# Attention and two MLP stages on one core: split fp32r products for batches 0 and 1 and for ten slots of block 0

## The chip, the cores and the metric

The kernel runs on one core of a Trainium2 chip. The metric is device time in microseconds (us), from launch to end; the median of three runs of the kernel before is 1787.25 us (1786.49 to 1788.84). The core's engines are named as in the profile: PE is TensorE's matrix multiply and PEld its weight load, DVE is VectorE, ACT is ScalarE, POOL is GpSimd, SP is the engine that issues most DMAs.

## What is computed

Three stages follow one another: attention over pooled keys and values (8 batches, 8 heads, 576 rows, head size 64; pooling by 8 leaves 72 keys), a first MLP with a cosine gate, and a second MLP with a SiLU gate.

```python
k_p = k.reshape(B, H, Sp, 8, D).mean(axis=3)
v_p = v.reshape(B, H, Sp, 8, D).mean(axis=3)
scores = q @ k_p.T / sqrt(D)                     # softmax over 72 keys
x = softmax(scores) @ v_p                        # to 4608 tokens x 512
h = x @ w_in;  x = (h * cos(h)) @ w_out          # 512 -> 2048 -> 512
g = x @ w_gate                                   # 512 -> 1536
out = (silu(g) * (x @ w_val)) @ w_out2           # 1536 -> 512
```

All inputs are float32 or float64 on the host and the output is float32. The MLP weights arrive as 64-bit words and are put together into float32 on the chip.

## The kernel before

**Two kinds of product.** A product in plain float32 is one matmul instruction, which the trace lists as two records. A split product writes each operand as a high part in fp32r (a rounded float32) and a low part, the remainder, and adds three matmuls: high by high, high by low, low by high. The high part is an ACT copy (`nc.scalar.copy`) and the low part a DVE subtraction.

**Blocks and slots.** The 4608 tokens are nine blocks of 512. Block n of the first MLP has 16 slots f, one for each 128 of the 2048 hidden rows. In a slot `pe_h` makes h with 12 split matmuls from `xhl` (the split input) and `wa` (split w_in), `turns` and `cosine` make g = h cos(h) in a tile `w` on ACT and DVE, `parts` splits g into `gh` and `gl` one slot later, and `pe_y` of two slots before adds g times w_out into four PSUM banks `acc`. A slot's h needs one of two PSUM banks, which the last DVE step of `cosine` (L573) two slots earlier frees. In block 0 the constant `Y32 = NF1 = 16` sends all slots down the plain path of `pe_y` (L599): four float32 matmuls from `w` and the float32 weights `wo_raw`, with no `parts`. From block 1 on `pe_y` has 12 split matmuls (L606 to L608), and `wo_high` (L553) and L586 make the split weights.

**Attention.** `do_s` makes scores, `do_pt` transposes the probabilities of a tile of 128 rows into `pth` (high), `ptl` (low) and `ptx` (the last 8 keys), `prep_v` makes the values' parts `vmh`, `vml`, `vl1`, `vl2`, and `do_av` multiplies them and ACT writes the result into `ring`. Batches below `ACTB = 2` take a plain float32 path: `do_av` has two float32 matmuls, `do_pt` no subtraction, `prep_v` no low parts. Later batches have five fp32r matmuls. Batch 0 is worked off ahead of the first slot (av of rows 0 to 511) and beside slots 0 and 1 (the last 64 rows); `x_split` makes `xhl` from `ring` as soon as it is there. Batch 1's attention runs beside slots 1 to 15, batch 2's beside block 1. Scores, transposes and av share the two PSUM banks tagged `att`.

**Weights and raw inputs.** `conv` turns the 64-bit words of w_in (tiles `st_i`, 16 of them) and w_out (`st_o`, 16) into float32: per tile one ACT scale (L477) and three DVE steps (L482, L487, L494), and for w_in a split (L1010 on ACT, L994 on DVE). It is called by `fill` all through the preamble and block 0. `load_kv1` loads batch 1's raw keys and values into tiles that belong to later weights: keys in `wa30` to `wa32`, values in `wa20` to `wa22`. DVE sums them (`pool_sum`, L213 and L215). SP issues all these loads in one order, and a load that waits for its tile holds up those behind it. Raw inputs of batch 2 and later are summed by POOL.

**Order.** The program is written slot by slot; a scheduler then sets each engine's order, except where `keep_in_program_order` pins an instruction (`x_split` of block 0, some transposes). Each engine works through its list strictly in that order.

Of the kernel before, what the change touches and what calls it, by code (L numbers as in the profile page):

```python
# [8 lines left out]
F32 = mybir.dt.float32  # L9
F32R = mybir.dt.float32r  # L10
# [15 lines left out]
def fused_kernel(  # L26
# [18 lines left out]
    nc = tc.nc  # L45
    B, H, S, D = q.shape
# [18 lines left out]
    PTW = 320  # L65
    LEAD = 4
    ACTB = 2
    Y32 = NF1

    const = ctx.enter_context(tc.tile_pool(name="const", bufs=1))  # L70
    chain = ctx.enter_context(tc.tile_pool(name="chain", bufs=2))
    dram = ctx.enter_context(tc.tile_pool(name="dram", bufs=1, space=bass.MemoryType.DRAM))
    psum = ctx.enter_context(tc.tile_pool(name="psum", bufs=1, space=bass.MemoryType.PSUM))
    wts = ctx.enter_context(tc.tile_pool(name="wts", bufs=1, reuse_waits="tile"))
    p1w = tc.alloc_tile_pool(name="p1w", bufs=2, side="right", reuse_waits="tile")
    p1a = tc.alloc_tile_pool(name="p1a", bufs=1, reuse_waits="tile")

    ident = const.tile([P, P], F32, name="ident")
# [5 lines left out]
    mask = few[:, 0]  # L84
# [20 lines left out]
    kT = p1a.tile([P, NP, 2 * SP], F32, name="kT")  # L105
    av_tiles = {}

    def av_tile(nm, b):

        kind = F32 if b < ACTB else F32R  # L110
        if (nm, kind) not in av_tiles:
            shape = {"v": [P, NP, P], "p": [P, NP, PTW], "x": [P, PTW]}["x" if nm == "ptx" else nm[0]]
            t = av_tiles[nm, kind] = p1a.tile(shape, kind, name=f"{nm}_{b}", tag=nm)
            if nm in ("vmh", "vml", "vl2"):
                nc.gpsimd.memset(t if kind is F32 else t.bitcast(F32), 0.0)
        return av_tiles[nm, kind]
# [50 lines left out]
    kraw1 = []  # L167
    vraw1 = []
# [19 lines left out]

    def load_kv1():

        for g in range(3):
            t = wts.tile([P, 2, TB], F32, name=f"k1_{g}", tag=f"wa3{g}")
            kraw1.append(t if g < 2 else t[: SL * NP])
            if g < 2:
                for x in range(2):
                    nc.sync.dma_start(t[x * SM : (x + 1) * SM], kview[1][g, x])
            else:
                for r in range(2):
                    nc.sync.dma_start(t[: SL * NP, r], kleft[1][r])
        for j in range(0, NP + 1, 2):  # L200
            t = wts.tile([P, 2, TB], F32, name=f"v1_{j}", tag=f"wa2{j // 2}")
            for r in range(2):
                rows = t[r * SM : (r + 1) * SM]
                if j < NP:
                    nc.sync.dma_start(rows, vview[1][r, :, j : j + 2])
                else:
                    nc.sync.dma_start(rows[:, 0], vleft[1])
            vraw1.append((j, t[:, : min(2, NP + 1 - j)]))

    def pool_sum(eng, dst, raw):  # L210
        h = POOL * D // 2
# [37 lines left out]
            nc.scalar.mul(to[:, :, SM:], ps[rows, 2 * P :].rearrange("d (s p) -> d p s", p=NP), -EXP_SCALE)  # L249

    def prep_v(b):
        vmh, vml, vl1, vl2 = (av_tile(nm, b) for nm in ("vmh", "vml", "vl1", "vl2"))
        vp = vps.pop(b)
        if b < ACTB:
            for r in range(2):
                rows, cols = slice(r * SM, (r + 1) * SM), slice(r * D, (r + 1) * D)
                nc.scalar.mul(vmh[rows, :, cols], vp[rows, :NP], 1.0 / POOL)
            nc.vector.tensor_mul(
                vl1[:SM].rearrange("q p (r d) -> q r p d", r=2),
                vp[:SM, NP : NP + 1].rearrange("q (a o) d -> q a o d", a=1).to_broadcast([SM, 2, NP, D]),  # L260
                mask[:SM].rearrange("q (p r o) -> q r p o", r=2, o=1).to_broadcast([SM, 2, NP, D]),
            )
            return
        for r in range(2):
            rows, cols = slice(r * SM, (r + 1) * SM), slice(r * D, (r + 1) * D)
            nc.scalar.mul(vmh[rows, :, cols], vp[rows, :NP], 1.0 / POOL)
            nc.vector.scalar_tensor_tensor(
                out=vml[rows, :, cols], in0=vp[rows, :NP], scalar=1.0 / POOL, in1=vmh[rows, :, cols],
                op0=ALU.mult, op1=ALU.subtract,
            )  # L270
        t = p1a.tile([P, H, SP], F32, name=f"vt_{b}", tag="e")[:, :, :D]
        nc.vector.tensor_mul(
            t, vp[:, NP : NP + 1].to_broadcast([P, H, D]), mask.rearrange("p (h o) -> p h o", o=1).to_broadcast([P, H, D])
        )
        t = t.rearrange("q (p r) d -> q r p d", r=2)
        h2 = vl1.rearrange("q p (r d) -> q r p d", r=2)
        l2 = vl2.rearrange("q p (r d) -> q r p d", r=2)
        for r in range(2):
            nc.scalar.copy(h2[:, r], t[:, r])
            nc.vector.tensor_sub(l2[:SM, r], t[:SM, r], h2[:SM, r])  # L280
# [49 lines left out]
    def do_norm(b, t, pm=None):  # L330
        n = TILES[t][1]
        e = es.pop((b, t))[:n]
        if b < ACTB:
            sm = sms.pop((b, t))[:n]
        else:
            sm = p1a.tile([P, H, 1], F32, name=f"sm_{b}_{t}", tag="sm", bufs=2)[:n]
            nc.vector.reduce_sum(sm[:, :, 0], e, axis=AX.X)
        nc.vector.tensor_scalar_add(sm, sm, 1e-9)
        nc.vector.reciprocal(sm, sm)
        if pm is None:  # L340
            pm = p1a.tile([P, H * SM + P], F32, name=f"pm_{b}_{t}", tag="pm")
        pms[b, t] = pm
        nc.vector.tensor_mul(
            pm[:n, : H * SM].rearrange("q (h s) -> q h s", h=H), e[:, :, :SM], sm.to_broadcast([n, H, SM])
        )

        for g in range(2):
            left = pm[:n, H * SM + g * SM : H * SM + (g + 1) * SM].rearrange("q (h s) -> q h s", h=H)
            if g == 0:
                nc.vector.tensor_mul(left, e[:, :, SM:], sm.to_broadcast([n, H, SL]))  # L350
            elif b >= ACTB:
                nc.vector.tensor_copy(pm[:n, H * SM + SM :], pm[:n, H * SM : H * SM + SM])

    def do_pt(b, t):
        pth, ptl, ptx = av_tile("pth", b), av_tile("ptl", b), av_tile("ptx", b)
        t0, n = TILES[t]
        o = t0 - GROUPS[GROUP[t]][0]
        pm = pms.pop((b, t))
        ps = psum.tile([P, NP, n], F32, name=f"pt_{b}_{t}", tag="att", bufs=2)
        for p in range(NP):  # L360
            pinned(nc.tensor.transpose(ps[:, p], pm[:n, p * P : (p + 1) * P], ident[:n, :n]), (b, t) == (0, 4))
        if b < ACTB:
            nc.scalar.copy(pth[:, :, o : o + n], ps)
            px = psum.tile([SM, n], F32, name=f"px_{b}_{t}", tag="att", bufs=2)
            nc.tensor.transpose(px, pm[:n, NP * P : NP * P + SM], ident[:n, :n])
            nc.scalar.copy(ptx[:SM, o : o + n], px)
            return
        nc.scalar.copy(pth[:, :, o : o + n], ps)
        nc.vector.tensor_sub(ptl[:, :, o : o + n], ps, pth[:, :, o : o + n])
        px = psum.tile([P, n], F32, name=f"px_{b}_{t}", tag="att", bufs=2)  # L370
        nc.tensor.transpose(px, pm[:n, NP * P :], ident[:n, :n])
        nc.scalar.copy(ptx[:, o : o + n], px)
        nc.vector.tensor_sub(ptx[SM:, o : o + n], px[SM:], ptx[SM:, o : o + n])

    def do_av(b, g, p):
        vmh, vml, vl1, vl2, pth, ptl, ptx = (
            av_tile(nm, b) for nm in ("vmh", "vml", "vl1", "vl2", "pth", "ptl", "ptx")
        )
        g0, n = (GROUPS if b else GROUPS0)[g]
        o = 256 if g == 2 else 0  # L380
        ps = psum.tile([P, n], F32, name=f"av_{b}_{g}_{p}", tag="att", bufs=2)
        terms = [
            (vmh, pth[:, p, o : o + n]),
            (vmh, ptl[:, p, o : o + n]),
            (vml, pth[:, p, o : o + n]),
            (vl1, ptx[:, o : o + n]),
            (vl2, ptx[:, o : o + n]),
        ]
        if b < ACTB:
            terms = [(vmh, pth[:, p, o : o + n])]  # L390
# [734 lines left out]
    for i, s in enumerate(slots):  # L1125
        n, f = s
# [157 lines left out]
```

## Time and profile before

| | us |
|---|---|
| median of three runs | 1787.25 |
| lowest, highest | 1786.49, 1788.84 |
| the profiled execution, its own time | 1786.07 |
| its span, first to last instruction | 1784.3 |
| PE busy | 1737.2 (97% of the span) |
| DVE busy | 1169.0 (66%) |
| ACT busy | 996.1 (56%) |
| POOL busy | 122.1 (7%) |

The profiled execution took 1.8 us more than its span. Busy times are instruction durations joined together; a PE matmul is shown from start to end, and the next one starts before it ends, so the distance between two starts tells more than a duration. PE idles for about 47 us of the span, nearly all of it in the first 130 us. The timelines list instructions of one engine with start, duration, line and tiles, and in brackets the idle time before one and what released it.

### The profile page before, as it was taken

To read this page: it belongs to the slowest core of one execution; us is meant where nothing else is said; L and a number is where in the kernel's file an instruction comes from. 1 tells how busy PE (TensorE), PEld (TensorE's weight loads), DVE (VectorE), ACT (ScalarE), POOL (GpSimd) and SP (SyncE) were. 2 spreads that over 40 slices of the span, in tenths; PEclk is the share of its full clock that TensorE was granted. 3 is DMA by queue.
4 is the path that set the end of the run, shared out by engine and by line. 5 is a ranking of instruction groups with operands and counts; after the bars stand their busy time and mean duration, and the time that the engine had idled before them with its cause. 6 is when DMAs were issued, how large, how long until landed. Compare 5 with 4: busy or idle time off the path is not lost.

```text
span 1784.3 us, 23241 instructions
## 1 busy us (share of the span) xinstructions
PE 1737.2 (97%) x8076; PEld 1444.5 (81%) x8076; DVE 1169.0 (66%) x2006; ACT 996.1 (56%) x1815; POOL 122.1 (7%) x217
## 2 busy tenths in 40 slices
PE   4979999999999999999999999999999999999998
PEld 3546588888888888888888778888888888999998
DVE  6695377867767677687675677853684377458346
ACT  5576477767667767677575565433443344344333
POOL 0131300403003011000000000000000000000000
PEclk9989999999999999999999999999999999999999
DMA  9553244646576455575775587675567657777772
GB/s 232 162 162 105 82 149 145 194 133 205 131 228 208 118 201 145 188 213 160 230 265 182 192 321 270 202 274 195 195 208 257 197 191 225 298 255 244 298 253 90
DMA packets 240244, 357.00 MB, mean 200 GB/s; under 512 B 141696, under 2 KB 147840, under 8 KB 240128
## 3 DMA queue, kind: packets, MB, share of 16 engines
q1 hardware_dynamic: 235440, 354.35, 61.5%
q10 hardware_dynamic: 4688, 1.18, 0.3%
q8 instruction: 64, 1.05, 0.2%
q14 instruction: 52, 0.43, 0.1%
HBM read 285.74 MB, written 69.73 MB: 199 GB/s over the span
## 4 chain that ended last, share of the span: by engine, by line
PE 89%; DMA 4%; DVE 4%; ACT 2%; issue 1%; POOL 0%; SPq 0%; ACTq 0%; DVEq 0%; POOLq 0%
PE X L791 14%; PE oX L921 8%; PE h L537 7%; PE h L538 7%; PE h L539 7%; PE acc L606 7%; PE Y L791 7%; PE acc L608 7%; PE acc L607 7%; PE oY L921 4%; PE av L393 3%; PE Z L791 3%; PE acc L599 2%; PE oZ L921 2%; PE s L308 2%; DMA w2r<-w_dram 1%
## 5 line engine op out<-in xcount | busy, mean ns | idle before, releaser
L791 PE MATMUL X<-t_P,wc 128*128 128x512 f32 (+1 forms) x1080 | 232.9, 368 | 2.3 <-ACT u L840 2.3
L537 PE MATMUL h<-xhl,wa 128*128 128x512 f32 x576 | 232.0, 403 | 1.3 <-DVE w L573 1.3
L539 PE MATMUL h<-xhl,wa 128*128 128x512 f32 x576 | 225.9, 392 | 0.0
L538 PE MATMUL h<-xhl,wa 128*128 128x512 f32 x576 | 225.9, 392 | 0.0
L791 PEld LDWEIGHTS X<-t_P,wc 128*128 128x128 f32 x1080 | 196.5, 188 | 29.1 <-ACT u L840 4.0
L606 PE MATMUL acc<-gh,wo_ring 128*128 128x512 f32 x448 | 179.3, 400 | 0.0
L607 PE MATMUL acc<-gl,wo_ring 128*128 128x512 f32 x448 | 174.8, 390 | 0.0
L608 PE MATMUL acc<-gh,wo_ring 128*128 128x512 f32 x448 | 174.8, 390 | 0.0
L547 ACT ACTIVATE w<-h,few 128x512 f32<-128x512 f32 x144 | 98.9, 687 | 121.3 <-PE h L539 121.0
L548 DVE SCALAR_TENSOR_TENSOR w<-w,h 128x512 f32<-128x512 f32 x144 | 98.2, 682 | 68.8 <-ACT w L547 68.5
L537 PEld LDWEIGHTS h<-xhl,wa 128*128 128x128 f32 x576 | 109.1, 189 | 27.8 <-issue 3.8
L573 DVE SCALAR_TENSOR_TENSOR w<-w,h 128x512 f32<-128x512 f32 x144 | 98.4, 683 | 49.9 <-ACT w L570 48.2
L538 PEld LDWEIGHTS h<-xhl,wa 128*128 128x128 f32 x576 | 108.9, 189 | 23.7 <-issue 2.4
L539 PEld LDWEIGHTS h<-xhl,wa 128*128 128x128 f32 x576 | 108.9, 189 | 23.0
L587 DVE TENSOR_TENSOR gl<-w,gh 128x512 fp32r<-128x512 f32 x128 | 90.9, 710 | 51.0 <-ACT gh L584 50.1
L584 ACT CAST gh<-w 128x512 fp32r<-128x512 f32 x128 | 78.9, 616 | 69.3 <-DVE w L573 47.3
L569 ACT ACTIVATE w<-w 128x512 f32<-128x512 f32 x144 | 91.1, 633 | 46.1 <-DVE w L548 45.1
L843 DVE TENSOR_TENSOR p<-p,X 128x512 f32<-128x512 f32 (+1 forms) x60 | 37.8, 632 | 116.8 <-PE X L791 108.6
L126 ACT CAST xhl<-pst 128x1024 fp32r<-128x1024 f32 (+1 forms) x70 | 67.7, 968 | 71.3 <-PE oX L921 26.1
L921 PE MATMUL oX<-xhl,wc 128*128 128x512 f32 (+1 forms) x480 | 102.7, 368 | 0.0
L608 PEld LDWEIGHTS acc<-gh,wo_ring 128*128 128x128 f32 x448 | 84.1, 188 | 18.6
L606 PEld LDWEIGHTS acc<-gh,wo_ring 128*128 128x128 f32 x448 | 84.2, 188 | 17.0 <-issue 0.8
(196 smaller groups left out, 3377.2 us busy)
## 6 DMA issues: line engine op xcount, KB each, us to landing
wc<-wc_dram SPq DMA_DIRECT2D x273, 512.0 KB
wo_ring<-wo_dram SPq DMA_DIRECT2D x112, 512.0 KB
wc_dram<-wc SPq DMA_DIRECT2D x42, 512.0 KB
wc_dram<-ow SPq DMA_DIRECT2D x42, 256.0 KB
y_dram<-yo SPq DMA_DIRECT2D x18, 512.0 KB
w_dram<-ce_w SPq DMA_DIRECT2D x36, 256.0 KB
st_i<-in_moe_w_in_dram SPq DMA_DIRECT2D x16, 512.0 KB
st_o<-in_moe_w_out_dram SPq DMA_DIRECT2D x16, 512.0 KB
```

Source lines behind the costliest of these rows:

```text
L537: nc.tensor.matmul(ps, whi, xhl[0][:, 0, c], start=c == 0, stop=False)
L538: nc.tensor.matmul(ps, whi, xhl[0][:, 1, c], start=False, stop=False)
L539: nc.tensor.matmul(ps, wlo, xhl[0][:, 0, c], start=False, stop=c == KC - 1)
L547: nc.scalar.activation(w, h, AF.Identity, bias=magic)
L548: nc.vector.scalar_tensor_tensor(out=w, in0=w, scalar=MAGIC, in1=h, op0=ALU.subtract, op1=ALU.subtract)
L569: nc.scalar.activation(w, w, AF.Sin, scale=PI)
L573: nc.vector.scalar_tensor_tensor(out=w, in0=w, scalar=1.0, in1=h, op0=ALU.subtract, op1=ALU.mult, reverse0=True)
L606: nc.tensor.matmul(acc[n][i], a[:, cols], xh, start=f == 0, stop=False)
L607: nc.tensor.matmul(acc[n][i], a[:, cols], xl, start=False, stop=False)
L608: nc.tensor.matmul(acc[n][i], b[:, cols], xh, start=False, stop=f == NF1 - 1)
L791: nc.tensor.matmul(ps[:, :hb], w, t[:, x, c, :hb], start=first and c == 0 and n == 0, stop=c == 1 and n == 2, skip_group_check=not first,)
L921: nc.tensor.matmul(banks[key][m][:, :hb], u, x[:, b, i, :hb], start=first_ and j == i == k == 0, stop=j == NJ - 1 and i == 1 and k == 2, s ...
```

## The change

`Y32` falls from 16 to 6: slots 6 to 15 of block 0 take the split path, with `wo_high`, `parts` and 12 matmuls each. The branches on `b < ACTB` go from `av_tile`, `prep_v`, `do_norm`, `do_pt` and `do_av`: batches 0 and 1 get the five-matmul av and all low parts. Their softmax keeps its own form. Batch 1's raw keys 0 and 1 move from `wa30` and `wa31` to the two `wo` buffers, and its values from `wa20` to `wa22` into the `gh` and `gl` buffers and `wa33`, one head pair a tile (ten loads of 128 KB in place of four of 256 and two of 128); the tiles `wo`, `gh` and `gl` are first written by `parts` of slot 6.

```diff
-    Y32 = NF1
+    Y32 = 6
@@ load_kv1
-        for g in range(3):
-            t = wts.tile([P, 2, TB], F32, name=f"k1_{g}", tag=f"wa3{g}")
...
+        for g in range(2):
+            t = p1w.tile([P, 2, TB], F32, name=f"k1_{g}", tag="wo", bufs=2)
...
+        t = wts.tile([P, 2, TB], F32, name="k1_2", tag="wa32")[: SL * NP]
...
-        for j in range(0, NP + 1, 2):
-            t = wts.tile([P, 2, TB], F32, name=f"v1_{j}", tag=f"wa2{j // 2}")
+        for j in range(NP + 1):
+            if j < NP:
+                t = chain.tile([P, 1, TB], F32, name=f"v1_{j}", tag="gh" if j < 2 else "gl", bufs=2)
             else:
+                t = wts.tile([P, 2, TB], F32, name=f"v1_{j}", tag="wa33")[:, :1]
@@ do_norm
-            elif b >= ACTB:
+            else:
                 nc.vector.tensor_copy(pm[:n, H * SM + SM :], pm[:n, H * SM : H * SM + SM])
@@ do_pt
-        if b < ACTB:
-            nc.scalar.copy(pth[:, :, o : o + n], ps)
-            px = psum.tile([SM, n], F32, name=f"px_{b}_{t}", tag="att", bufs=2)
-            nc.tensor.transpose(px, pm[:n, NP * P : NP * P + SM], ident[:n, :n])
-            nc.scalar.copy(ptx[:SM, o : o + n], px)
-            return
         nc.scalar.copy(pth[:, :, o : o + n], ps)
         nc.vector.tensor_sub(ptl[:, :, o : o + n], ps, pth[:, :, o : o + n])
@@ do_av
-        if b < ACTB:
-            terms = [(vmh, pth[:, p, o : o + n])]
-            terms += [(vl1[:SM], ptx[:SM, o : o + n])]
```

**PE, around the second product of slot 6.** Before, between batch 1's scores of tile 3 and h of slot 9:

```order
L308 MATMUL s_3_0_1062<-kT,qT_3_902 128x144 x2
L308 MATMUL s_3_1_1072<-kT,qT_3_902 128x144 x2
L599 MATMUL acc_0_696<-w_6_945,wo_449 128x512
L599 MATMUL acc_1_697<-w_6_945,wo_449 128x512
L599 MATMUL acc_2_698<-w_6_945,wo_449 128x512
L599 MATMUL acc_3_699<-w_6_945,wo_449 128x512
L293 MATMUL qp_4_1082<-ident,q_453 128x64 x4
```

After, from the same scores to the second of the four banks (the third and fourth follow in the same way; L586 to L588 are L606 to L608 of before):

```order
L297 MATMUL s_3_0_1172<-kT,qT_3_983 128x144 x2
L297 MATMUL s_3_1_1182<-kT,qT_3_983 128x144 x2
L586 MATMUL acc_0_766<-gh_6_1086,wo_6_1088 128x512
L587 MATMUL acc_0_766<-gl_6_1087,wo_6_1088 128x512
L588 MATMUL acc_0_766<-gh_6_1086,wo_6_1088 128x512
L586 MATMUL acc_1_767<-gh_6_1086,wo_6_1088 128x512
L587 MATMUL acc_1_767<-gl_6_1087,wo_6_1088 128x512
L588 MATMUL acc_1_767<-gh_6_1086,wo_6_1088 128x512
```

Four float32 matmuls from `w` and the raw weights became twelve fp32r matmuls from `gh`, `gl` and `wo`.

**DVE, in batch 0's attention ahead of the first slot.** Before, from the normalization of tile 1 (its probabilities lie in `vst`) to the score minima of tile 3:

```order
L343 TENSOR_TENSOR vst<-vst,sm_1_240 128x512
L350 TENSOR_TENSOR vst<-vst,sm_1_240 128x64
L494 SCALAR_TENSOR_TENSOR ce_i_0_193<-st_i_0_161,ce_i_0_193 128x512
L482 TENSOR_SCALAR ce_i_1_261<-ce_i_1_261 128x512
L338 TENSOR_SCALAR sm_2_279<-sm_2_279 128x8
L482 TENSOR_SCALAR ce_i_2_329<-ce_i_2_329 128x512
L487 SCALAR_TENSOR_TENSOR ce_i_1_261<-st_i_1_163,ce_i_1_261 128x512
L994 TENSOR_TENSOR wa_0_333<-ce_i_0_193,wa_0_333 128x512
L494 SCALAR_TENSOR_TENSOR ce_i_1_261<-st_i_1_163,ce_i_1_261 128x512
L312 TENSOR_REDUCE mx_3_0_348<-s_3_0_345 128x4
```

After, the same stretch from its copy on:

```order
L341 COPY vst<-vst 128x64
L974 TENSOR_TENSOR wa_0_352<-ce_i_0_199,wa_0_352 128x512
L467 SCALAR_TENSOR_TENSOR ce_i_1_267<-st_i_1_163,ce_i_1_267 128x512
L327 TENSOR_SCALAR sm_2_286<-sm_2_286 128x8
L462 TENSOR_SCALAR ce_i_2_348<-ce_i_2_348 128x512
L352 TENSOR_TENSOR ptl<-pt_1_337,pth 128x4x128
L356 TENSOR_TENSOR ptx<-px_1_344,ptx 64x128
L474 SCALAR_TENSOR_TENSOR ce_i_1_267<-st_i_1_163,ce_i_1_267 128x512
L328 RECIPROCAL sm_2_286<-sm_2_286 128x8
L301 TENSOR_REDUCE mx_3_0_367<-s_3_0_364 128x4
```

Two subtractions that read the transposed tile in its `att` bank now stand ahead of the score minima of tile 3, whose scores need a bank of the same tag.

**SP, behind batch 1's raw values.** Before (`k`, `v` are batch 1's raw tiles, `st_i` raw w_in, `q` batch 1's queries):

```order
L205 DMA v_0_176<-in_v_dram 64x2x512 x2
L205 DMA v_2_179<-in_v_dram 64x2x512 x2
L207 DMA v_4_182<-in_v_dram 64x1x512 x2
L470 DMA st_i_3_337<-in_moe_w_in_dram 128x512
L470 DMA st_i_0_451<-in_moe_w_in_dram 128x512
L159 DMA q_453<-in_q_dram 128x8x64 x4
```

After:

```order
L206 DMA v_2_182<-in_v_dram 64x512 x2
L206 DMA v_3_185<-in_v_dram 64x512 x2
L206 DMA v_4_188<-in_v_dram 64x1x512 x2
L450 DMA st_i_3_356<-in_moe_w_in_dram 128x512
L450 DMA st_i_0_500<-in_moe_w_in_dram 128x512
L158 DMA q_502<-in_q_dram 128x8x64 x4
```

The order is the same, but the second `st_i` load goes to `wa20`, which held `v_0` before and now holds nothing.

## Rows read from the trace of the kernel before

**Rows 1.** Busy us (and counts) of PE, PEld, DVE, ACT, POOL, granted clock, DMA.

```profile
46.50:70.20 23.70, 22.67 (x46) 11.09 (x47) 11.55 (x30) 9.16 (x27) 0.00 (x0) 1.00 0.60 161
...
85.60:126.50 40.90, 28.83 (x99) 17.37 (x99) 39.54 (x69) 31.67 (x82) 15.29 (x22) 0.92 0.43 140
...
149.85:222.80 72.95, 72.95 (x257) 43.81 (x256) 31.49 (x60) 41.98 (x101) 17.96 (x34) 1.00 0.29 77
222.80:1784.30 1561.50, 1554.07 (x7454) 1331.33 (x7452) 1029.87 (x1742) 861.64 (x1451) 72.62 (x128) 1.00 0.63 207
```

**Rows 2.** PE timeline ahead of slot 0: start, duration, line, tiles, [idle and releaser].

```profile
38.85 2.29 PE L308 MATMUL s<-kT,qT 128*128 128x144 f32 x8 [0.46 <-ACT pth L363]
...
46.55 1.19 PE L393 MATMUL av<-pth,vmh 128*128 128x256 f32 x2 [0.79 <-issue]
...
59.36 1.22 PE L393 MATMUL av<-pth,vmh 128*128 128x256 f32 x2 [0.52 <-ACT pth L363]
...
68.56 0.79 PE L537 MATMUL h<-xhl,wa 128*128 128x512 f32 x1
69.16 0.63 PE L538 MATMUL h<-xhl,wa 128*128 128x512 f32 x1
69.58 0.63 PE L539 MATMUL h<-xhl,wa 128*128 128x512 f32 x1
```

**Rows 3.** PE timeline, its two longest idle stretches in block 0.

```profile
97.92 6.11 PE L599 MATMUL acc<-w,wo 128*128 128x512 f32 x8 [7.12 <-DVE wo L494]
...
126.55 1.03 PE L293 MATMUL qp<-ident,q 128*128 128x128 f32 x4 [4.29 <-ACT e L318]
```

**Rows 4.** PE timeline, one plain slot of block 0, one split slot of block 1.

```profile
171.40 3.60 PE L599 MATMUL acc<-w,wo 128*128 128x512 f32 x8
...
177.60 0.38 PE L242 MATMUL kps<-ident,kp 128*128 128x128 f32 x2
...
222.77 0.39 PE L606 MATMUL acc<-gh,wo 128*128 128x512 f32 x1
...
228.21 1.14 PE L308 MATMUL s<-kT,qT 128*128 128x144 f32 x8
```

**Rows 5.** PE timeline, av of batch 1 and of batch 2, two at a time.

```profile
137.67 0.59 PE L393 MATMUL av<-pth,vmh 128*128 128x256 f32 x2
...
140.08 3.70 PE L599 MATMUL acc<-w,wo 128*128 128x512 f32 x8
...
191.20 0.70 PE L393 MATMUL av<-pth,vmh 128*128 128x320 f32 x2
...
194.03 3.70 PE L599 MATMUL acc<-w,wo 128*128 128x512 f32 x8
...
253.22 0.28 PE L393 MATMUL av<-pth,vmh 128*128 128x256 f32 x1
...
254.41 0.40 PE L606 MATMUL acc<-gh,wo 128*128 128x512 f32 x1
```

**Rows 6.** DVE timeline, steps of the split path in block 1.

```profile
226.34 0.69 DVE L586 TENSOR_TENSOR wo<-wo,wo 128x512 fp32r<-128x512 f32 x1 [0.56 <-ACT wo L553]
226.95 0.68 DVE L573 SCALAR_TENSOR_TENSOR w<-w,h 128x512 f32<-128x512 f32 x1
...
236.69 0.68 DVE L369 TENSOR_TENSOR ptl<-pt,pth 128x512 fp32r<-128x512 f32 x1
237.40 0.29 DVE L373 TENSOR_TENSOR ptx<-px,ptx 64x128 fp32r<-64x128 f32 x1
```

**Rows 7.** DVE timeline: slot 1's cosine, a step beside POOL, slot 5's cosine.

```profile
85.59 0.67 DVE L573 SCALAR_TENSOR_TENSOR w<-w,h 128x512 f32<-128x512 f32 x1
...
107.67 1.22 DVE L487 SCALAR_TENSOR_TENSOR wo<-st_o,wo 128x512 uint32<-128x512 uint32 x1
...
133.37 0.68 DVE L573 SCALAR_TENSOR_TENSOR w<-w,h 128x512 f32<-128x512 f32 x1
```

**Rows 8.** Waits of SP's queue, 0 to 240 us: us in total, times, longest.

```profile
SPq L470 <- DVE v L213: 13.8, 1, 13.8
```

More of the change, by code (lines that the diff above doesn't have):

```diff
@@ L106, in fused_kernel, with av_tile @@
     av_tiles = {}
-    def av_tile(nm, b):
-        kind = F32 if b < ACTB else F32R
-        if (nm, kind) not in av_tiles:
+    def av_tile(nm):
+        if nm not in av_tiles:
             shape = {"v": [P, NP, P], "p": [P, NP, PTW], "x": [P, PTW]}["x" if nm == "ptx" else nm[0]]
-            t = av_tiles[nm, kind] = p1a.tile(shape, kind, name=f"{nm}_{b}", tag=nm)
+            t = av_tiles[nm] = p1a.tile(shape, F32R, name=nm)
             if nm in ("vmh", "vml", "vl2"):
-                nc.gpsimd.memset(t if kind is F32 else t.bitcast(F32), 0.0)
-        return av_tiles[nm, kind]
+                nc.gpsimd.memset(t.bitcast(F32), 0.0)
+        return av_tiles[nm]
     nc.gpsimd.memset(kT, 0.0)
     for nm in ("vmh", "vml", "vl1", "vl2", "pth", "ptl", "ptx"):
-        av_tile(nm, 0)
+        av_tile(nm)
     def raw_tile(nm):
@@ L189, in load_kv1 @@
     def load_kv1():
-        for g in range(3):
-            t = wts.tile([P, 2, TB], F32, name=f"k1_{g}", tag=f"wa3{g}")
[L193 to L196, printed above, removed]
-            else:
-                for r in range(2):
-                    nc.sync.dma_start(t[: SL * NP, r], kleft[1][r])
-        for j in range(0, NP + 1, 2):
-            t = wts.tile([P, 2, TB], F32, name=f"v1_{j}", tag=f"wa2{j // 2}")
+        for g in range(2):
+            t = p1w.tile([P, 2, TB], F32, name=f"k1_{g}", tag="wo", bufs=2)
+            kraw1.append(t)
+            for x in range(2):
+                nc.sync.dma_start(t[x * SM : (x + 1) * SM], kview[1][g, x])
+        t = wts.tile([P, 2, TB], F32, name="k1_2", tag="wa32")[: SL * NP]
+        kraw1.append(t)
+        for r in range(2):
+            nc.sync.dma_start(t[:, r], kleft[1][r])
+        for j in range(NP + 1):
+            if j < NP:
+                t = chain.tile([P, 1, TB], F32, name=f"v1_{j}", tag="gh" if j < 2 else "gl", bufs=2)
+            else:
+                t = wts.tile([P, 2, TB], F32, name=f"v1_{j}", tag="wa33")[:, :1]
             for r in range(2):
                 rows = t[r * SM : (r + 1) * SM]
[L204 to L208, printed above, removed]
+                nc.sync.dma_start(rows, vview[1][r, :, j : j + 1] if j < NP else vleft[1])
+            vraw1.append((j, t))
     def pool_sum(eng, dst, raw):
@@ L251, in prep_v @@
     def prep_v(b):
-        vmh, vml, vl1, vl2 = (av_tile(nm, b) for nm in ("vmh", "vml", "vl1", "vl2"))
+        vmh, vml, vl1, vl2 = (av_tile(nm) for nm in ("vmh", "vml", "vl1", "vl2"))
         vp = vps.pop(b)
-        if b < ACTB:
[L255 to L262, printed above, removed]
-            return
         for r in range(2):
@@ L350, in do_norm @@
                 nc.vector.tensor_mul(left, e[:, :, SM:], sm.to_broadcast([n, H, SL]))
-            elif b >= ACTB:
+            else:
                 nc.vector.tensor_copy(pm[:n, H * SM + SM :], pm[:n, H * SM : H * SM + SM])
     def do_pt(b, t):
-        pth, ptl, ptx = av_tile("pth", b), av_tile("ptl", b), av_tile("ptx", b)
+        pth, ptl, ptx = av_tile("pth"), av_tile("ptl"), av_tile("ptx")
         t0, n = TILES[t]
@@ L361, in do_pt @@
             pinned(nc.tensor.transpose(ps[:, p], pm[:n, p * P : (p + 1) * P], ident[:n, :n]), (b, t) == (0, 4))
-        if b < ACTB:
-            nc.scalar.copy(pth[:, :, o : o + n], ps)
-            px = psum.tile([SM, n], F32, name=f"px_{b}_{t}", tag="att", bufs=2)
-            nc.tensor.transpose(px, pm[:n, NP * P : NP * P + SM], ident[:n, :n])
-            nc.scalar.copy(ptx[:SM, o : o + n], px)
-            return
         nc.scalar.copy(pth[:, :, o : o + n], ps)
@@ L376, in do_av @@
         vmh, vml, vl1, vl2, pth, ptl, ptx = (
-            av_tile(nm, b) for nm in ("vmh", "vml", "vl1", "vl2", "pth", "ptl", "ptx")
+            av_tile(nm) for nm in ("vmh", "vml", "vl1", "vl2", "pth", "ptl", "ptx")
         )
@@ L388, in do_av @@
         ]
-        if b < ACTB:
-            terms = [(vmh, pth[:, p, o : o + n])]
-            terms += [(vl1[:SM], ptx[:SM, o : o + n])]
         for i, (w, x) in enumerate(terms):
```

## The prediction

> **What bounds the kernel now.** I read the busy times by stretch first [rows 1]. From 222.8 us to the end PE is busy 1554 of 1561.5 us: nothing but PE work counts there. The instruction orders of all engines are the same there but for the first slots of block 1, so whatever block 0 gains or loses reaches the end unchanged. From 149.85 to 222.8 (the second product of slot 6 to the end of block 0) PE is busy all the time, with DVE at 31.5 and ACT at 42 of 73 us. So a PE microsecond saved there is saved, as long as DVE and ACT can follow. From 85.6 to 126.5 it is different: DVE is busy 39.5 of 40.9 us, PE 28.8. DVE converts weights there, and PE waits for it, 7.1 us ahead of the first plain product and 4.3 us ahead of a transpose of batch 1's queries [rows 3]. From 46.5 to 70.2 PE works through batch 0's av, and DVE is half idle.
>
> PE's clock matters twice. At 69.16 and 69.58 two matmuls of 512 columns start 0.42 us apart [rows 2], which is the lower level, 1.2 GHz (the window's granted clock of 1.00 doesn't show it); the eight records after the 7.1 us wait take 6.11 us [rows 3] where eight others take 3.60 [rows 4].
>
> **Ten split slots.** A plain slot with its h runs from 171.40 to 177.60, 6.20 us. A split one of block 1 runs from 222.77 to 228.21, 5.44 us [rows 4]. That is 0.76 us less a slot, and 7.6 us for ten; slots 6 to 15 all lie in the stretch that PE bounds. Each adds an ACT copy of the weights and one of g, and two DVE subtractions, 0.61 us from start to start [rows 6]: 12 us of DVE and some 11 of ACT in all.
>
> **Batch 1's av.** Two products of 256 columns take 2.41 us plain (137.67 to 140.08) and 1.19 split (253.22 to 254.41); two of 320 take 2.83 plain (191.20 to 194.03) [rows 5], and 1.49 split if 1.19 is scaled by the columns. Two such pairs of each: 2 x 1.22 + 2 x 1.34 = 5.1 us, all under PE's bound. Each of the five tiles adds two DVE steps to `do_pt` (0.68 and 0.29, [rows 6]) and a short copy, about 1 us a tile.
>
> **Batch 0, ahead of slot 0.** Here PE gains and DVE costs. Group 1's av takes 59.36 to 68.56, 9.2 us [rows 2], group 0's the same from 46.55. Split, a product of 256 columns is 0.60 us at the full clock [rows 5], so 1.2 at 1.2 GHz and 4.8 for four. That would be 8.8 us less for the two groups. Against it: DVE's list ahead of tile 3's minima now has the subtractions of tiles 0 and 1, two copies and the values' low parts (four half-width steps and one full in place of one full). By [rows 6] these are about 3.5 us, in a part where DVE has little slack. And the `att` bank of tile 1's transpose, which ACT's copy freed before (38.85, [rows 2]), is now freed by DVE. So tile 3's scores move from 38.85 to about 42.4, group 0's av from 46.55 to 50 and its end from 55.75 to 55. Between the groups the same bank rule puts two more subtractions in line, 1.2 us on top of the 3.6 from 55.75 to 59.36. Group 1 then runs from 59.7 to 64.5 and h begins 4 us earlier than at 68.56. Bounds: 0 if DVE falls 4 us further behind, 8.8 if all of it finds idle DVE time.
>
> The loads help here. SP waited 13.8 us for DVE to be done with batch 1's first value tile before it could load into `wa20` [rows 8], with batch 1's queries and all later weights behind it. That tile is free now, so conversions can fill DVE time that was idle between 46.5 and 85.6. Ten value loads and fifteen sums in place of six and nine cost DVE about half a microsecond, ahead of `x_split`, whose subtractions wait for group 1's av anyway.
>
> **From slot 0 to slot 5.** Of the 4 us I carry 2 to slot 1's cosine (85.59, [rows 7]): in the new ACT order slot 0's sine stands behind slot 1's h, and h at 1.2 GHz takes 12 x 0.42 = 5 us. From there to slot 5's cosine (133.37) DVE sets the pace. Counted in the two orders from `x_split` to batch 1's third minima, DVE has 93 instructions where it had 82, priced by durations of the trace 1.7 us more; but 3.4 us more of the list lie ahead of slot 1's cosine. So 1.7 us less remain, and the minima come 2 + 1.7, say 4 us earlier. Behind them hangs the transpose at 126.55 [rows 3]. In the new PE order ten matmuls of h of slot 6 and one of slot 4's product stand ahead of that transpose, not behind it: about 3 us of PE work move into its wait. That makes 7. I take off 1, because slot 3's cosine comes late in DVE's new list, slot 5's h needs its bank, and PE may idle long enough to fall to 1.2 GHz again, at 2.5 us a time as in [rows 3]. So 6 us up to there, between 0 and 11.
>
> **Does DVE keep up?** After slot 5's cosine DVE has some 30 us of work by its list up to slot 9's `gl`, PE about 31 us up to the product that needs it. That is a tie, and I take off 0.7 us. From slot 10 on DVE has about 20 us of work against PE's 44.
>
> The Trainium skill has a rule against the added steps. What the trace shows first: a conversion step took 1.22 us at 107.67 [rows 7], beside POOL's sums, where such a step takes 0.69. The page "SBUF — State Buffer" (section "SBUF: two separate sides") says that a VectorE instruction with both inputs in SBUF and a GpSimd one that reads SBUF exclude each other, and the new `gl` and weight subtractions have both inputs there. Were all twenty to collide, DVE would have 10.6 us more; POOL is busy 18 of 73 us there, which makes it nearer to 2.6.
>
> **The sum.** 6 + 5.1 + 7.6 - 0.7 = 18 us. Against the profiled execution's own 1786.07 us (span 1784.3 and 1.8 around it) that is 1768; the median of the runs is 1.2 above it, so I predict 1769.
>
> **The rivals.**
> - *Nothing is gained ahead of slot 6.* DVE's extra work in batch 0's attention eats what av saves, and the transpose's wait stays. Against it stand 23.7 us in which DVE worked 11.6 [rows 1]. Left are 5.1 + 7.6: 1774.5. Chance 0.15.
> - *DVE bounds slots 6 to 15.* From 85.59 to 133.37 DVE took 47.8 us [rows 7] for a list of 37, 1.29 times as long, through waits and POOL. At 1.4 times, its list of 51 us from slot 5's to slot 15's cosine takes 71 us where PE needs 60: 11 us lost, partly covered by the tail of block 0, so about 7 and 1776. For it: the conversions run into those slots now. Against it: POOL is quieter there. Chance 0.17.
> - *All of it is gained.* Av ahead of slot 0 gives 8.8 and the transpose's wait 3; with 12.7 that is 24: 1763. Chance 0.15.
> - *Slower: PE falls to 1.2 GHz in split slots.* Both long idle stretches were followed by slow matmuls [rows 3]. If h of each slot waits more than 4 us for the cosine that frees its bank, the slot's 24 matmuls at 0.42 take 10.1 us, not 5.44: 4.7 us lost a slot, plus the wait. Four such slots use up the 18 us, six give some 1797. Against it: it needs DVE behind by 4 us in slot after slot, and the tie above leaves waits of a microsecond. Chance 0.04.
>
> **How the numbers follow.** My forecast has 0.49. The range of 1762 to 1778 holds it and the first three rivals, with the scatter of each; outside are the slow case and the worst of a bound DVE. A change of 0.2%, 3.6 us, is about what a measurement of this kernel can tell from none. All cases but the last are faster by more: faster 0.94, same 0.02, slower 0.04.
>
> **What would show it.** PE's h of slot 0 beginning near 64.5; the first split product near 141 in place of 149.85; then slots of 5.4 us of matmul without idle time; block 1's first product near 205 in place of 222.77, and everything behind it shifted as a whole. Wrong would be: idle time of PE ahead of h in slots 6 to 10 released by L573's successor (DVE too slow), or group 1's av starting after 62 (DVE's subtractions dearer than I think), or block 1 and later longer than 1561 us.

## The result, and the profile after

The changed kernel takes 1767.05 us (median of 4 runs, 1765.35 to 1767.73) where the kernel before, run beside it, takes 1786.95 (1786.49 to 1788.84). The ratio is 0.9885 with a 95% interval of 0.9868 to 0.9902: 19.9 us less, where 18 were forecast.

First the stretches of the changed kernel that answer to [rows 1]. The cuts are at DVE's cosine of slot 0 (73.70), of slot 5 (120.05), the first split product, which is slot 6's (137.84), and block 1's first product (203.04). Columns: busy time and count of PE, PEld, DVE, ACT, POOL, then granted clock, DMA share, GB/s.

```profile
44.00:73.70 29.70, 21.06 (x105) 16.23 (x104) 27.11 (x70) 21.55 (x70) 3.39 (x5) 1.00 0.75 230
73.70:120.05 46.35, 40.32 (x145) 28.18 (x146) 41.21 (x78) 35.35 (x84) 19.34 (x27) 0.85 0.37 113
120.05:137.84 17.79, 16.78 (x77) 11.42 (x76) 17.59 (x34) 14.92 (x40) 5.33 (x7) 1.00 0.47 157
137.84:203.04 65.20, 63.80 (x301) 51.59 (x300) 49.40 (x89) 51.96 (x120) 21.26 (x33) 1.00 0.41 112
203.04:1764.40 1561.36, 1553.86 (x7454) 1331.47 (x7452) 1031.04 (x1743) 863.26 (x1452) 73.88 (x128) 1.00 0.64 208
```

The same cuts in the kernel before:

```profile
44.00:80.10 36.10, 33.99 (x97) 18.95 (x95) 18.40 (x45) 17.79 (x54) 0.00 (x0) 1.00 0.64 194
80.10:133.40 53.30, 40.60 (x149) 26.34 (x150) 48.75 (x86) 42.72 (x107) 22.22 (x30) 0.90 0.43 139
133.40:149.85 16.45, 16.45 (x60) 9.94 (x60) 12.85 (x21) 8.04 (x16) 4.87 (x7) 1.00 0.52 168
149.85:222.77 72.92, 72.92 (x257) 43.78 (x256) 31.46 (x60) 41.98 (x101) 17.96 (x34) 1.00 0.29 77
```

Slot 6's product starts 12.0 us earlier (149.85 to 137.84). The stretch from there to block 1 is 7.7 us shorter (72.92 to 65.20). Everything behind it lasts 1561.4 us, where it lasted 1561.5 [rows 1]. So all of the gain lies in block 0, three fifths of it ahead of the first split slot.

In the first line DVE is busy 27.1 of 29.7 us and PE 21.1. In the same part of the kernel before DVE was busy 18.4 of 36.1 us and PE 34.0. PE does not wait less: from 44 us to slot 6's product it is idle for 15.7 us (the first three lines), where it was idle for 14.8. Its busy time there fell from 91.0 to 78.2 us. So the 12.0 us are, in amount, PE's own time; its waits moved, and did not get shorter in sum.

PE's timeline of the changed kernel at the rows that answer to [rows 2] (start, duration, line, tiles, idle time and releaser):

```profile
50.26 0.55 PE L373 MATMUL av<-pth,vmh 128*128 128x256 f32 x1 [0.78 <-issue]
...
53.71 0.35 PE L373 MATMUL av<-pth,vmh 128*128 128x256 f32 x1
53.90 0.28 PE L373 MATMUL av<-ptl,vmh 128*128 128x256 f32 x1
54.02 0.28 PE L373 MATMUL av<-pth,vml 128*128 128x256 f32 x1
...
58.68 0.38 PE L373 MATMUL av<-pth,vmh 128*128 128x256 f32 x1 [1.47 <-DVE ptl L352]
58.90 0.28 PE L373 MATMUL av<-ptl,vmh 128*128 128x256 f32 x1
...
62.55 0.50 PE L518 MATMUL h<-xhl,wa 128*128 128x512 f32 x1 [0.52 <-DVE xhl L496]
62.89 0.40 PE L519 MATMUL h<-xhl,wa 128*128 128x512 f32 x1
63.13 0.39 PE L517 MATMUL h<-xhl,wa 128*128 128x512 f32 x1
```

Group 1's av is done at 61.6. All but the first two matmuls of h of slot 0 run from 62.55 us on, 0.23 us apart, where they were 0.42 apart in [rows 2]. The first plain product and five of PE's waits in what follows answer to [rows 3]:

```profile
86.43 3.60 PE L579 MATMUL acc<-w,wo 128*128 128x512 f32 x8
...
101.19 0.66 PE L282 MATMUL qp<-ident,q 128*128 128x128 f32 x4 [1.31 <-ACT e L307]
105.35 1.11 PE L350 MATMUL pt<-ident,pm 128*128 128x128 f32 x4 [3.51 <-ACT e L307]
...
107.87 0.80 PE L517 MATMUL h<-xhl,wa 128*128 128x512 f32 x1 [1.19 <-DVE w L553]
...
121.47 0.66 PE L282 MATMUL qp<-ident,q 128*128 128x128 f32 x4 [0.70 <-ACT e L307]
...
142.73 0.46 PE L282 MATMUL qp<-ident,q 64*128 64x64 f32 x4 [1.40 <-ACT e L307]
```

The wait of 7.12 us ahead of the first plain product is gone: that product starts at 86.43, 11.5 us earlier. Of the 4.29 us ahead of the queries' transpose 0.70 are left (121.47). But three waits between them, of 1.31, 3.51 and 1.19 us, are new.

### The profile page after: what moved, and what is told of

The parts are those of the page before. It is cut to its first block, busy times and chain, and to the rows that moved or that the text cites. A ratio compares the mean times of both kernels' runs of the same rounds, so it can differ in the third digit from the quotient of the medians.

```text
span 1764.4 us, 23443 instructions
## 1 busy us (share of the span) xinstructions
PE 1712.9 (97%) x8136; PEld 1451.5 (82%) x8136; DVE 1194.8 (68%) x2070; ACT 1008.9 (57%) x1839; POOL 126.7 (7%) x214
## 4 chain that ended last, share of the span: by engine, by line
PE 89%; DMA 5%; DVE 3%; ACT 1%; SPq 1%; issue 0%; POOL 0%; ACTq 0%; DVEq 0%; POOLq 0%
PE X L771 15%; PE oX L901 8%; PE Y L771 7%; PE acc L586 7%; PE h L517 7%; PE h L519 7%; PE h L518 7%; PE acc L588 7%; PE acc L587 7%; PE oY L901 4%; PE Z L771 4%; PE av L373 2%; PE oZ L901 2%; PE s L297 2%; DMA st_i<-in_moe_w_in_dram 1%; DMA w2r<-w_dram 1%
## 5 line engine op out<-in xcount | busy, mean ns | idle before, releaser
L586 PE MATMUL acc<-gh,wo_ring 128*128 128x512 f32 x448 | 179.3, 400 | 0.0
L588 PE MATMUL acc<-gh,wo_ring 128*128 128x512 f32 x448 | 174.7, 390 | 0.0
L527 ACT ACTIVATE w<-h,few 128x512 f32<-128x512 f32 x144 | 98.9, 687 | 105.9 <-PE h L519 104.7
L567 DVE TENSOR_TENSOR gl<-w,gh 128x512 fp32r<-128x512 f32 x138 | 97.0, 703 | 50.5 <-ACT gh L564 49.6
L564 ACT CAST gh<-w 128x512 fp32r<-128x512 f32 x138 | 85.1, 617 | 73.1 <-DVE w L553 51.6
L125 ACT CAST xhl<-pst 128x1024 fp32r<-128x1024 f32 (+1 forms) x70 | 67.7, 968 | 71.3 <-PE oX L901 26.1
L588 PEld LDWEIGHTS acc<-gh,wo_ring 128*128 128x128 f32 x448 | 84.1, 188 | 18.6
L586 PEld LDWEIGHTS acc<-gh,wo_ring 128*128 128x128 f32 x448 | 84.2, 188 | 17.0 <-issue 0.8
```

The lines of the kernel that those rows point to most:

```text
L527: nc.scalar.activation(w, h, AF.Identity, bias=magic)
L567: nc.vector.tensor_sub(b, w, a)
L586: nc.tensor.matmul(acc[n][i], a[:, cols], xh, start=f == 0, stop=False)
L588: nc.tensor.matmul(acc[n][i], b[:, cols], xh, start=False, stop=f == NF1 - 1)
```

## The experiments

The change has three parts: the split av of batches 0 and 1, the ten split slots, and batch 1's raw keys and values in other tiles. Theory 1 is the prediction's: the parts add up, and PE's shorter work carries the gain. Theory 2 is that the loads carry what is gained ahead of slot 6, since the moved raw tiles free SP of its 13.8 us wait [rows 8]. A third question came up on the way: is it DVE's pace that carries it? The kernel before, run beside each of them, took a median of 1786.73 to 1787.67 us.

**Split av alone**: the changed kernel with load_kv1 as in the kernel before, and all slots plain.

```diff
-    Y32 = 6
+    Y32 = NF1
```

> The split av of batches 0 and 1 alone: all sixteen output slots of block 0 stay plain and batch 1's raw keys and values stay in the tiles of before. Theory 1 (av carries the gain ahead of slot 6): group 1's av ends about 6 us earlier, as in the changed kernel, the DVE work behind it moves up with it, and batch 1's four products save 5.1 us: about 1776 us. Theory 2 (the loads carry it): SP still waits for DVE ahead of batch 1's queries and the later weights, so what av gains in front is lost again in PE's wait ahead of the first plain product, and only the 5.1 us remain: about 1782 us.

1774.14 us, ratio 0.992 (0.9907 to 0.9934): 13.1 us less. Theory 2 falls, since the loads were as before and SP's wait was there (13.3 us).

**Raw tiles alone** (the kernel before with the new load_kv1).

> The raw keys and values of batch 1 in the tiles of later split parts alone: products of batches 0 and 1 plain, sixteen plain output slots. Theory 1: SP's 13.8 us wait goes, but group 1's av still ends where it did and DVE sets the pace behind it: 0 to 2 us less, about 1786 us. Theory 2: DVE's conversions move into the time of batch 0's av, the 7.1 us wait ahead of the first plain product goes and most of the 4.3 us ahead of the queries' transpose: 7 us less or more, about 1779 us.

1789.25 us, ratio 1.0013 (1.0004 to 1.0022): 2 us more. The move brings nothing by itself. The waits of SP's queue (in total, times, longest) tell why. This is the first row for the kernel before, then for this one:

```profile
SPq L470 <- DVE wo L494: 41.9, 12, 13.6
```

```profile
SPq L470 <- DVE wo L494: 52.9, 14, 22.6
```

The wait for a value tile went. The next load then waits longer for its staging buffer, which a conversion step on DVE frees. So the free tile did not bring the loads forward: DVE held them one load later.

**Ten split slots alone.**

```diff
-    Y32 = NF1
+    Y32 = 6
```

> Ten split output slots alone (slots 6 to 15 of block 0), the rest as before. If PE bounds those slots: 10 x 0.76 us less, about 1779.5 us, with PE without idle time from slot 6 on. If DVE bounds them (its steps take 1.3 to 1.4 times their list there): 0 to 3 us less, about 1785 us, with idle time of PE ahead of h in slots 6 to 10.

1780.52 us, ratio 0.9961 (0.9948 to 0.9973): 6.7 us less. From slot 6's product to block 1:

```profile
151.59:217.91 66.32, 66.32 (x297) 50.98 (x296) 44.54 (x77) 51.24 (x119) 21.54 (x34) 1.00 0.36 97
```

PE is busy in all of its 66.3 us, 6.6 less than 72.92: 0.66 us a slot, not 0.76. Ahead of it 1.7 us are lost (149.85 to 151.59), so that 4.9 arrive at block 1 (222.77 to 217.91).

**The changed kernel without the moved raw tiles.**

> The changed kernel with batch 1's raw keys and values in the tiles of before: split av and ten split slots. Theory 1: within 1 us of the changed kernel, about 1768 us. Theory 2: the load wait is back and costs about 7 us: about 1774.5 us, with several us of PE idle ahead of the first plain product.

1765.85 us, ratio 0.988 (0.9867 to 0.9894), not to be told from the changed kernel. This settles theory 2 from the other side.

**Split av of batch 0 alone.** In prep_v, do_norm, do_pt, do_av and the choice of tiles, the plain path is kept for batch 1:

```diff
-        if b < ACTB:
+        if b == 1:
```

> Split av of batch 0 alone; batch 1's av plain, sixteen plain output slots, raw tiles of before. If the gain of the av split adds up by batches, this is what is left of the 13.1 us of both batches after the 5.1 us of batch 1: about 8 us, 1779 us, with slot 0's h some 6 us earlier than at 68.56 and all of it carried to slot 6. If DVE's pace behind slot 0 gives part of it back, as the prediction had it (2 of 4 us carried, 4 us left at slot 5): 2 to 4 us, 1783 to 1785 us.

1774.67 us, ratio 0.9932 (0.992 to 0.9945): 12.1 us less, more than was left over for it. Its stretches with the same cuts as above (slot 0's and slot 5's cosine, slot 6's product, block 1):

```profile
44.00:73.30 29.30, 22.66 (x105) 18.02 (x104) 25.58 (x64) 21.02 (x68) 0.00 (x0) 0.94 0.55 162
73.30:121.80 48.50, 41.07 (x161) 26.87 (x161) 47.14 (x82) 42.29 (x108) 28.00 (x40) 0.96 0.60 192
121.80:137.56 15.76, 15.28 (x58) 9.49 (x57) 11.49 (x22) 8.06 (x16) 2.21 (x3) 1.00 0.68 217
137.56:210.49 72.93, 72.93 (x257) 43.78 (x256) 31.27 (x60) 41.80 (x100) 17.54 (x34) 1.00 0.28 74
```

The gain is 6.8 us at slot 0's cosine, 11.6 at slot 5's and 12.3 at slot 6's product, and it stays 12.3. In between it is not even: 0.3 at slot 1's cosine (85.27 for 85.59), which now has more conversions ahead of it in DVE's list, and 3.1, 1.5 and 11.4 at those of slots 2 to 4.

PE is busy 79.0 us in the first three lines, where it was busy 91.0, and idle 14.6, where it was idle 14.8. So the 12.3 us are nearly the 12.0 us of PE time that the split av saves, 11.3 of them ahead of slot 0's cosine. There PE loses 4.5 of these to new waits (6.6 us idle for 2.1); from there to slot 5's cosine it waits 5.3 us less (7.4 for 12.7).

The longest of the later waits ended with a step of DVE [rows 3]. From 44 us to slot 6's product DVE does 84.2 us of work in 93.6, where before it did 80.0 in 105.9. It has 4.2 us more to do and 16.5 us less idle time (9.4 in place of 25.9), and 14 of these lie ahead of slot 0's cosine. DVE's timeline shows which. In the kernel before:

```profile
62.84 0.69 DVE L516 TENSOR_TENSOR xhl<-ring,xhl 128x512 fp32r<-128x512 f32 x1 [6.55 <-ACT xhl L515]
65.14 0.69 DVE L516 TENSOR_TENSOR xhl<-ring,xhl 128x512 fp32r<-128x512 f32 x1 [1.61 <-ACT xhl L515]
...
69.59 1.29 DVE L516 TENSOR_TENSOR xhl<-ring,xhl 128x512 fp32r<-128x512 f32 x2 [2.70 <-ACT xhl L515]
...
80.09 0.69 DVE L573 SCALAR_TENSOR_TENSOR w<-w,h 128x512 f32<-128x512 f32 x1 [2.99 <-ACT w L570]
...
97.18 0.69 DVE L494 SCALAR_TENSOR_TENSOR wo<-st_o,wo 128x512 uint32<-128x512 uint32 x1
```

With batch 0's av split:

```profile
62.83 0.67 DVE L517 TENSOR_TENSOR xhl<-ring,xhl 128x512 fp32r<-128x512 f32 x1
63.77 1.29 DVE L517 TENSOR_TENSOR xhl<-ring,xhl 128x512 fp32r<-128x512 f32 x2 [0.27 <-ACT xhl L516]
65.23 0.69 DVE L517 TENSOR_TENSOR xhl<-ring,xhl 128x512 fp32r<-128x512 f32 x1 [0.17 <-ACT xhl L516]
...
73.29 0.69 DVE L574 SCALAR_TENSOR_TENSOR w<-w,h 128x512 f32<-128x512 f32 x1
...
83.66 1.10 DVE L495 SCALAR_TENSOR_TENSOR wo<-st_o,wo 128x512 uint32<-128x512 uint32 x1
```

And PE's first plain product there:

```profile
84.81 3.70 PE L600 MATMUL acc<-w,wo 128*128 128x512 f32 x8 [1.30 <-DVE wo L495]
```

DVE stood at x_split until the slow av was copied out, piece by piece, with its conversions of weights queued behind. With the faster av the last step of x_split comes 5.0 us earlier (it is the second of the two at 69.59), the conversions move up behind it, and the one that the first plain product waited for runs at 83.66 in place of 97.18. That product starts at 84.81 in place of 97.92.

**Split av of batch 1 alone** (the same edit with `b < 1`).

> Split av of batch 1 alone; batch 0 as before, sixteen plain output slots. By the term of the sum: 2 x 1.22 + 2 x 1.34 = 5.1 us less, about 1782 us, since PE's products lie behind the last wait of block 0. Rival: the ten DVE steps and the copies that it adds (about 1 us a tile) fall into the stretch where DVE is busy nearly all the time and eat 3 to 5 us of it: 1785 to 1787 us.

1781.09 us, ratio 0.9966 (0.9954 to 0.9979): 5.6 us less. In the trace slot 6's product comes 1.6 us earlier (148.29), and the stretch behind it, with group 1's av, is 2.9 us shorter (69.98 to block 1). Beside batch 0's it is worth far less. In the traces batch 0 alone has slot 6's product at 137.56, and both batches have it at 139.49, 1.9 us later, though group 0's products save 2.4 us of PE's time. From slot 0's cosine to there PE is idle for 10.9 us with both batches and for 7.9 with batch 0 alone. That the added steps on DVE cause this is likely and not shown. Of the 2.9 us behind slot 6 this leaves 1.0 in all. The medians say the same (12.1 and 13.1), but the intervals of the two ratios overlap. How the gain is shared out also depends on the order: added to batch 1's split, batch 0's is worth 8.8 us (block 1 from 218.27 to 209.48), not 12.3.

**More work for DVE in front.** In do_pt of the changed kernel:

```diff
         nc.vector.tensor_sub(ptl[:, :, o : o + n], ps, pth[:, :, o : o + n])
+        if b == 0 and t < 4:
+            nc.vector.tensor_sub(ptl[:, :, o : o + n], ps, pth[:, :, o : o + n])
```

> The changed kernel with the subtraction that makes ptl written twice for the four tiles of 128 queries of batch 0: four more DVE steps of 0.68 us, 2.7 us in all. If DVE's list in front of the scores and of av is on the path (PE's waits there end with ptl in the changed kernel): slot 0's h begins 2 to 2.7 us later and the end as much later, about 1769.5 us. If DVE has slack there: within 0.5 us of the changed kernel, 1767 us.

1767.93 us, ratio 0.9888 (0.9875 to 0.9902). Group 1's av starts 3.5 us later (62.20), slot 6's product 4.3 us later (142.14). But the stretch from there to block 1 then takes 63.1 us, not 65.2, and PE no longer idles in it. The profiled span is 2.2 us longer, the median 0.9, and the intervals overlap. So DVE's list in front is on the path to group 1's av. How much of the 4.3 us is DVE's this run doesn't tell, because TensorE's clock differed too. Group 1's av ran at 1.2 GHz, its matmuls 0.21 us apart, where they were 0.12 apart in the changed kernel:

```profile
64.16 0.41 PE L375 MATMUL av<-ptl,vmh 128*128 128x256 f32 x1
64.37 0.41 PE L375 MATMUL av<-pth,vml 128*128 128x256 f32 x1
```

From 44 us to slot 6's product PE is busy 80.9 us for 78.2, and idle 17.2 for 15.7. Half of the delay at slot 6 is made up behind it, and what arrives at the end is too small for these runs to size.

**Two more split slots** (raw tiles of before, `Y32 = 4`).

> Split av and split output slots from slot 4 on (twelve in place of ten), batch 1's raw keys and values in the tiles of before. If PE bounds slots 4 and 5 too: 2 x 0.76 us less than with ten, about 1764.5 us. If DVE bounds ahead of slot 6: its four more subtractions of about 0.65 us come on top instead, 2.6 us more at the most, 1766 to 1768.5 us.

1764.48 us, ratio 0.9872 (0.9857 to 0.9887): 1.4 us less than with ten, near the forecast, but the two intervals overlap. It is the fastest kernel of the study, 2.6 us below the changed one, and not shown to be faster.

**Conversions in DVE's idle time**, with av plain, once with the moved raw tiles and once without:

```diff
-        "s0 s1 f4 x0 s2 p0 V0 v x1 p1 f6 s3 s4 F3 a0 x2 p2 x3 p3 a1 w i1 q G2 K0 K1 K2 U0 X i11 o2 "
-        "x4 b f6 "
+        "s0 s1 f4 x0 s2 p0 V0 v x1 p1 f6 s3 s4 F3 a0 x2 p2 x3 p3 a1 w i1 q G2 K0 K1 K2 U0 f4 X i11 o2 "
+        "x4 b f2 "
```

> No part of the split: av and output slots plain. Batch 1's raw keys and values in the tiles of later split parts, and four conversion steps of weights written ahead of x_split in DVE's order instead of behind it, where DVE of the kernel before stands idle for 6.55 us until av is done. If that idle time is what cost the kernel before (DVE later sets the pace up to slot 5): 4 to 7 us less than before, about 1782 us, though av is as slow as it was. If av's own duration on PE is what counts: no gain, 1787 us.

> The same four conversion steps ahead of x_split, with batch 1's raw keys and values in the tiles of before, so that SP waits 13 us for DVE ahead of the weights that these steps convert. If the loads then arrive too late, DVE waits for them ahead of x_split and slot 0 starts later: 1787 us or more. If they arrive in time: as with the moved raw tiles, about 1782 us.

1787.46 us (ratio 0.9999, 0.999 to 1.0008) and 1787.22 us (0.9997, 0.9988 to 1.0005): no gain in either. This doesn't decide the question, because the idle time was not filled. DVE's timeline of the first of the two at the first moved step:

```profile
64.61 0.43 DVE L482 TENSOR_SCALAR ce_i<-ce_i 128x512 uint32<-128x512 uint32 x1 [8.18 <-ACT ce_i L477]
```

The step needs ACT's scaling of the same tile, and that stands in ACT's order behind the first two copies of the results of group 1's av. So the conversions waited for av too, x_split came behind them (73.97 in place of 62.84), and slot 0's cosine at 86.03 in place of 80.09. PE's wait ahead of the first plain product is gone here as well (it starts at 91.33), but one ahead of slot 0's h is new:

```profile
73.41 1.22 PE L537 MATMUL h<-xhl,wa 128*128 128x512 f32 x2 [5.20 <-ACT xhl L515]
```

Slot 6's product came 1.2 us earlier (148.63), with PE idle for 15.2 us from 44 us up to there. So the end of the 7.1 us wait is not by itself worth its length, and a slot 0 that is 6 us late need not cost anything at slot 6, here with more conversions done by then.

**Sums of batch 1 on POOL** in the kernel with twelve split slots, the values', then the keys' too:

```diff
-            pool_sum(nc.vector, vps[1][:, j : j + t.shape[1]], t)
+            pool_sum(nc.gpsimd, vps[1][:, j : j + t.shape[1]], t)
```

> The kernel of twelve split slots (raw tiles of before) with batch 1's value sums on POOL in place of DVE: nine steps, about 4.5 us, leave DVE's list ahead of x_split; POOL is idle there. If DVE's list up to slot 5 sets the time: 2 to 4 us less, 1761 to 1762 us. If it is hidden: 1764.5 us. If POOL's use of the memory slows DVE's steps beside it, or its later sums come late: up to 1767 us.

> The same with batch 1's key sums on POOL too, nine steps and about 4.5 us more off DVE's list. If DVE's list sets the time: 1758 to 1761 us. If POOL is then late for the transposes of the keys behind slot 0's h, slots 0 to 2 start later: 1765 us or more.

1768.2 us (ratio 0.989, 0.9876 to 0.9903) and 1770.4 us (0.9904, 0.9891 to 0.9918): 3.7 and 5.9 us more than without, though the interval of the first overlaps that of the kernel without. The groups of DVE's instructions from 30 to 62 us show a cause (busy time, mean ns of one, idle time before them). First the kernel with the sums on DVE:

```profile
L467 DVE SCALAR_TENSOR_TENSOR ce_i<-st_i,ce_i 128x512 uint32<-128x512 uint32 x5 | 3.4, 680 | 0.0
L352 DVE TENSOR_TENSOR ptl<-pt,pth 128x512 fp32r<-128x512 f32 x4 | 2.8, 690 | 1.4 <-ACT pth L351 1.3
```

With both sums on POOL:

```profile
L467 DVE SCALAR_TENSOR_TENSOR ce_i<-st_i,ce_i 128x512 uint32<-128x512 uint32 x4 | 4.2, 1047 | 0.0
L352 DVE TENSOR_TENSOR ptl<-pt,pth 128x512 fp32r<-128x512 f32 x2 | 1.4, 688 | 0.0
```

A conversion step takes 1.05 us beside POOL, where it takes 0.68 alone. The subtraction that reads one input from PSUM is not slowed. What DVE gave away it lost again in its other steps (it is busy 29.3 of these 32 us, for 28.8 with the sums), and group 1's av started at 66.08 in place of 59.34.

## Why the prediction was right, and where its steps were not

The time (1769 for 1767.05) and the sign were right. Of the terms two were well off, in opposite directions, so that the time came out so near is partly luck.

- **Ten split slots, 7.6 us.** Measured 6.6, alone (72.92 to 66.32, though 4.9 at block 1) and on top of the split av (block 1 from 209.48 to 202.92). The mechanism held; 0.76 a slot should have been 0.66. Why is not shown.
- **Batch 0, 6 us with bounds 0 and 11.** Measured 12.3 alone, outside the bounds, and 8.8 on top of batch 1's, inside them. The first half of the working held: tile 3's scores came at 43.07 (forecast 42.4), av at 50.26 (50), group 1 at 58.68 (59.7). The clock term was too dear for the changed kernel: the four products of group 1, with a matmul of h among them, took 3.0 us (58.68 to 61.64), not 4.8, and h of slot 0 came at the full clock. With the split av alone they ran at 1.2 GHz and took 4.9 (58.61 to 63.47), as forecast. The step that failed is "of the 4 us I carry 2 to slot 1's cosine". That cosine came 6.1 us earlier in the changed kernel (79.51) and 0.3 with batch 0 alone, where 12.3 still arrived at slot 6: what arrives is not set there. I saw DVE's idle time ahead of x_split only as cover for new steps, and gave no term to the 7.1 us wait of [rows 3], although its releaser, a conversion on DVE, stood in that row. DVE's conversions moved up with x_split, and this wait and most of the 4.3 us one went, so that the time which PE lost to DVE ahead of slot 0 (4.5 us with batch 0 alone) came back behind it (5.3), where I had given it up.
- **Batch 1's av, 5.1 us.** Right alone (4.5 in the trace, 5.6 in the medians), but 1.0 beside batch 0's. PE waits 3.0 us more ahead of slot 6 there, probably for the ten added DVE steps, while I had called it PE's bound. Firmer than either share is the sum of the two av terms: 13.3 (block 1 from 222.77 to 209.48), where 11.1 stood.
- **The loads, no term, but named as the help that lets conversions fill idle time.** Wrong: by itself the move cost 2 us, and without it the change is as fast.
- **DVE keeping up, 0.7 us.** PE idles 1.4 of 65.2 us from slot 6 on, nearly all at the transpose at 142.73, and 0.1 without the moved raw tiles. The rival of a DVE that bounds slots 6 to 15 did not come true. Nearest to it are the 18 us ahead of slot 6, where DVE is busy 17.6 and PE idles 1.0.
- **The rule against the added subtractions** (the Trainium skill, "SBUF — State Buffer", section "SBUF: two separate sides"). From 121 to 206 us 24 steps of this kind take 0.69 us in the median; five take 0.8 to 1.2, together 1.6 us over it. That is below the 2.6 us that I leaned to. Where POOL sums most of the time (19.2 of 32 us, both sums on POOL), the trace agrees with the rule: a conversion step took 1.05 us for 0.68, and the step with one input in PSUM was not slowed.

By the sum: 12.3 for 6, 1.0 for 5.1 and 6.6 for 7.6 make 19.9 where 18 (with the 0.7) stood. In this order the two av terms miss by 6.3 and by 4.1 us, and they cancel in part because both use the same stretch ahead of slot 6. The signs at the end held: slot 6's product at 137.84 for "near 141", block 1's at 203.04 for "near 205", and nothing changed behind it.

Shown by runs: what each part is worth alone, and that the raw tiles are worth nothing. Shown by the trace of a run: that work added to DVE in front delays group 1's av. Only read from traces: that DVE's idle time at x_split is how batch 0's slow av cost time behind slot 0. The run meant to fill that time another way did not fill it. A plainer reading fits as well. In the traces of both kernels and of the first ten runs PE is idle for 13.3 to 17.4 us from 44 us to slot 6's product, while its busy time there goes from 77.5 to 93.0 us. By that, what counts ahead of slot 6 is PE's own time, clock included. No run takes the two readings apart.

## What to carry to other kernels

When engine A waits for B in one stretch and B for A in the next, a microsecond taken from A's work in the first may be lost there to a new wait for B and still arrive, because B, free earlier, ends a later wait of A sooner. Here it came to about one for one (12.0 us of PE time, 12.3 us gained). So look in B's list for what is queued behind its wait, and whose wait that work ends later, and add up A's idle time over both stretches before calling a wait gone. Two parts that use the same stretch need not add; measure them together. A load that waits for a buffer is not helped by another buffer when the next wait in its queue is for the same engine.

## What was not expected of the hardware

- TensorE's clock rose earlier with the split av. In the kernel before, h's matmuls were 0.42 us apart until 71.3 (the lower level, 1.2 GHz), 0.23 from 72.1 on, after 12 us of work without a wait. In the changed kernel the matmuls of 256 columns were 0.21 apart from 50.26 and 0.12 from 53.9 on, after 3.6 us of work. With batch 0 alone split, the same products, started 0.07 us later, stayed at 0.21 to their end, and the rise came at 62.4. Two kernels with the same PE work in this place differed in it, which no view here explains. With both batches split and the raw tiles of before it came at 53.0 with ten split slots and at 64.4 with none.
- DVE steps with one small input suffered beside POOL too: the three `sm` steps of 128x8 took 0.69 us on average with both sums on POOL, and 0.16 with the sums on DVE.
